# Attention and two feed-forward layers on one core: two small inputs stand behind the keys, and SyncE issues nearly all loads

## The chip, the cores and the metric

The kernel runs on one core of a Trainium2 chip. Its time is the device time of one execution in microseconds (us); lower is better. Five engines work side by side, each through its own instructions in order: TensorE (PE; PEld is its weight load), VectorE (DVE), ScalarE (ACT), GpSimd (POOL) and SyncE (SP). Transfers between HBM and on-chip memory are issued by an engine's queue (SPq, ACTq) and carried by 16 DMA engines.

## What is computed

```python
# q, k, v: batch 2, 8 heads, 768 positions, 64 wide; n_sink = 4, window = 128
scores = q @ k.T / 8                 # per head
keep = (col < n_sink) | ((0 <= row - col) & (row - col < window))
a = softmax(where(keep, scores, -1e9))
x = (a @ v) as 1536 tokens x 512
h = x @ moe_w_in                     # 512 -> 2048
x = (maximum(h, 0) + alpha * minimum(h, 0)) @ moe_w_out
x = maximum(x @ moe2_w_in, 0) ** 2 @ moe2_w_out      # again 512 -> 2048 -> 512
```

`n_sink`, `window` (the run's two numbers) and `alpha` are inputs of the run.

## The kernel before

Tokens are cut into 12 chunks of 128 (6 to a batch). Attention runs as 24 jobs, two to a chunk (`g`: four heads each). A job is: scores on TensorE (L529), mask and minimum on VectorE (L542), exponentials on ScalarE (L546), normalising (L562 on VectorE or L561 on ScalarE), transposes (L571), sums with the values (L604), and the result split into a high and a low fp32r part in `X` (L240, L247). The masks are made once, in `masks()`, from `parf`, the float copy of the run's two numbers.

A weight tile (`w`) is a half of 512 columns; packed it is 512 KB. The keys of a chunk are 320 KB, its values 256 KB, its queries 256 KB (or 128 KB a job). It arrives packed in a `raw` buffer (or in a part of `Y0` that serves as one), is unpacked by VectorE (L285, L287, L290) with a correction from ScalarE (L281), and split into `w`'s two parts (L240, L247). The first eight input halves (`w0` to `w7`) are wanted while attention runs; the feed-forward products of the first layer (L309, L341) begin between attention jobs. Both layers' products follow to the end.

`Plan` takes every step with a due number, its reads and writes and an estimated cost for each engine that could do it, and lists the steps by simulating that; each engine then runs its own list in order. `Plan({...})` at L694 holds the time at which each engine is thought to be free first, and each transfer carries a cost (the `"dma"` numbers). Transfers signal on eight semaphores that are taken in turn, and a transfer is issued only when the one that had its semaphore before has landed. So a queue (and the engine whose queue it is) can stand still ahead of a transfer.

Before, the keys of the first four chunks and the first two weight halves are issued by ScalarE (L276, L512), the rest by SyncE. `par` (two 64-bit numbers, copied to 128 partitions) and `alpha` are transfers of their own (L426, L707). Until the products begin, 34 identity products (`WARM`, L712) are spread over TensorE's list.

Of the kernel before, what the change touches and what calls it, by code (L numbers as in the profile page):

```python
# [8 lines left out]
F32 = mybir.dt.float32  # L9
# [9 lines left out]
P = 128  # L19
# [150 lines left out]
@with_exitstack  # L170
def attn_moe_moe(ctx, tc, q, k, v, vsink, par, alpha, w1, w2, out):
    nc = tc.nc
# [19 lines left out]
    const = pool_of(ctx, "const")  # L192
    al = const.tile([P, NF], F32, name="al")
    oma = const.tile([P, NF], F32, name="oma")
    flag = const.tile([1, 8], F32, name="flag")
    slow = const.tile([1, 1], I32, name="slow")
    parf = const.tile([P, 4], F32, name="parf")
    pari = const.tile([P, 4], I32, name="pari")
    X = const.tile([P, 2, KT, NTOK], F32R, name="X")
# [52 lines left out]
    class Feed:  # L252
# [9 lines left out]
        def half(self, due, layer, f, slot, a, need):  # L262
            add, new = self.plan.add, self.places.new
            wk = f"w{slot}_{a}"
            w = self.w[layer, f, a] = new(wk)
            q = self.halves
            self.halves += 1
            r, more = self.raws(q)
            early = RAW_LOADS[q:q + 1] if self.early else ()
            rk, ck, xk = f"raw{r}", f"cs{q % 2}", f"x{q % 2}"  # L270
            cs, x = new(ck), new(xk)
            raw = new(rk) if r < 4 else lambda: Y[0][:, (r - 4) * 1024:(r - 3) * 1024].bitcast(U32).rearrange(
                "p (j w) -> p j w", w=2)
            src = (w1, w2)[layer][f, :, a * 512:(a + 1) * 512].bitcast(U32).rearrange("p (j w) -> p j w", w=2)
            at = due - PARTS + a
            by = nc.scalar if early and q < 2 else nc.sync  # L276
            add(early[0] if early else due - LOAD + a, more, [rk], ("dma", 1456, lambda: by.dma_start(out=raw(), in_=src)))
# [122 lines left out]
    class Short:  # L400
# [18 lines left out]
        def masks(self):  # L419
            con = self.con  # L420
            self.K = [con.tile([P, NG, 2, KC], F32, name=f"K{i}") for i in range(4)]
            self.early = self.places.new("g7")

            self.queries(0)
            self.keys(0, 0, nc.scalar)
            nc.sync.dma_start(out=pari, in_=par.bitcast(I32).rearrange("(o n) -> o n", o=1).to_broadcast([P, 4]))  # L426
            self.ident = con.tile([P, P], F32, name="ident")
# [21 lines left out]
            nc.vector.scalar_tensor_tensor(out=mrel, in0=past, scalar=float(P), in1=rel, op0=ALU.mult, op1=ALU.add)  # L449
            nc.vector.tensor_copy(out=parf, in_=pari)  # L450
            nc.vector.tensor_scalar(nosink, col, ns_f, None, op0=ALU.is_ge)
# [4 lines left out]
            nc.vector.scalar_tensor_tensor(out=self.mask0, in0=past2, scalar=BIG, in1=nosink,  # L456
                                           op0=ALU.mult, op1=ALU.mult)

            def others():
# [22 lines left out]
        def keys(self, i, place, by):  # L482
            by.dma_start(out=self.K[place].rearrange("p g a n -> p g (a n)"), in_=k[divmod(ORDER[i], NCH)])

# [3 lines left out]
        def values(self, due, at, key, src):  # L488
            t = self.places.new(key)
            self.load(due, [key], t, src, 728)  # L490
            self.v[at] = t, key

        def job(self, i, b, c, g):
# [9 lines left out]
            if i < 4:  # L503
                qk, qt = ("g", 7, i // 2, 0), lambda: halves(self.early()[:, i // 2, g * 256:g * 256 + 256].bitcast(F32))
                if g == 0:
                    add(due - AHEAD, [], [qk, ("g", 7, i // 2, 2)], ("dma", 690, lambda: i and self.queries(i // 2)))
            else:
                qk, qt = ring("q", 2)
                self.load(due - AHEAD, [qk], qt, halves(q[b, c, :, g]), 364)
            if g == 0:  # L510
                add(due - AHEAD, [], [("K", here)], ("dma", 862, lambda: i and self.keys(
                    i // NG, here, nc.scalar if i < 4 else nc.sync)))  # L512
                self.values(VALUE_LOADS.get(ci, due - 4), (b, c), f"v{here}", v[b, c * P:(c + 1) * P, :])
# [9 lines left out]
            def scores():  # L523
                for p in range(2):

                    for x, y, at in ((0, KC, before), (KC, W3, here)) if c else ((0, P, here),):
                        for j in range(2):
                            rows = slice(j * D, (j + 1) * D)
                            nc.tensor.matmul(s()[:, 2 * p + j, x:y], lhsT=qt()[rows, p], rhs=K[at][rows, g, p, 0:y - x],  # L529
                                             start=True, stop=True)  # L530
# [84 lines left out]
    def full_attention():  # L615
        with ExitStack() as ctx:
# [22 lines left out]
            for c in range(NCH):  # L639
# [9 lines left out]
                for b in range(B):  # L649
                    for h in range(2 * 4):  # L650
# [6 lines left out]
                        for cc in range(NCH):  # L657
                            nc.sync.dma_start(out=kt[:, cc * P:(cc + 1) * P],
                                              in_=k[b, cc, :, g].rearrange("p (a s) -> p a s", a=2)[rows, pr % 2, 0:P])
                            nc.sync.dma_start(out=vv[:, cc], in_=v[b, cc * P:(cc + 1) * P, pr * 2 * D:(pr + 1) * 2 * D])  # L660
# [32 lines left out]
    with tc.manual_schedule():  # L693
        plan = Plan({"pe": 2500, "dve": 4500, "pool": 1500, "act": 2100, "dma": 800})  # L694
        places = Places()
# [10 lines left out]
        att.masks()  # L706
        plan.add(0, [], ["al"], ("dma", 56, lambda: nc.sync.dma_start(out=al, in_=alpha)))  # L707
        plan.add(0, ["al"], ["oma"], ("dve", 85, lambda: nc.vector.tensor_scalar(oma, al, -1.0, 1.0, op0=ALU.mult, op1=ALU.add)))
        att.start()
# [151 lines left out]
```

## Time and profile before

| | |
|---|---|
| median of 3 runs | 638.97 us (638.12 to 639.36) |
| the profiled execution | 638.03 us, of which 636.3 us are its span |
| TensorE busy | 618.6 us, 97% of the span |
| VectorE, ScalarE, GpSimd busy | 388.8, 253.0, 29.1 us |
| granted TensorE clock, mean | 0.993 |

The span runs from the first to the last instruction; 1.7 us of the execution lie outside it. The rows below come from the profiled execution, and their times count from the start of the span. A product on TensorE is pipelined and its end is modelled, so "busy" says only that TensorE had one under way.

### The profile page before, as it was taken

How to read it: one execution, taken by the hardware profiler on the slowest of the kernel's cores; microseconds unless marked ns; L12 is line 12 of the kernel's file. 1: busy time of each engine (PE TensorE's matmuls, PEld its weight loads, DVE VectorE, ACT ScalarE, POOL GpSimd, SP SyncE). 2: the span in 40 equal slices, each digit the busy share in tenths (PEclk: the TensorE clock that was granted, in tenths of full speed). 3: DMA queues.
4: the chain of work that ended last, by engine and by line, in shares of the span. 5: the costliest groups of instructions: out<-in, count | busy, mean ns of one | idle time of the engine just before them, and what ended most of it. 6: DMA issues, size and time to landing. Idle time of an engine off the chain costs nothing.

```text
span 636.3 us, 9094 instructions
## 1 busy us (share of the span) xinstructions
PE 618.6 (97%) x3448; PEld 512.7 (81%) x3448; DVE 388.8 (61%) x924; ACT 253.0 (40%) x591; POOL 29.1 (5%) x48
## 2 busy tenths in 40 slices
PE   5989999999999999999999999999999999999996
PEld 4778877878888888788888888888888888888885
DVE  3999997667755949554289993333396424434342
ACT  2888985556654725321045671111262201010110
POOL 0012112121100000000000000000000000000000
PEclk9889999999999999999999999999999999999999
DMA  8465233210262435200005540000040000100102
GB/s 311 163 237 172 85 100 93 92 39 26 79 221 66 133 98 167 67 1 1 0 4 176 193 141 18 1 0 1 0 133 1 2 0 1 67 0 21 46 1 71
DMA packets 18340, 48.13 MB, mean 76 GB/s; under 512 B 2288, under 2 KB 5104, under 8 KB 18288
## 3 DMA queue, kind: packets, MB, share of 16 engines
q1 hardware_dynamic: 17568, 45.63, 21.7%
q10 hardware_dynamic: 720, 1.84, 0.7%
q8 instruction: 29, 0.48, 0.3%
q14 instruction: 23, 0.19, 0.1%
HBM read 44.31 MB, written 3.15 MB: 75 GB/s over the span
## 4 chain that ended last, share of the span: by engine, by line
PE 88%; DVE 9%; DMA 2%; ACT 0%; issue 0%; SPq 0%; DVEq 0%
PE h L309 38%; PE yb L341 31%; PE h L341 10%; PE o L604 4%; PE s L529 3%; PE t L571 1%; DMA raw<-w 1%; DVE x L290 1%; DVE sp L542 1%; DVE w L247 1%; DVE r L321 1%; DVE x L287 1%; PE h L712 1%; DMA v<-v 1%; DVE g L247 1%; DVE s L536 1%
## 5 line engine op out<-in xcount | busy, mean ns | idle before, releaser
L309 PE MATMUL h<-X,w 128*128 128x512 f32 (+1 forms) x1248 | 275.1, 375 | 0.1
L309 PEld LDWEIGHTS h<-X,w 128*128 128x128 f32 x1248 | 221.6, 188 | 42.4 <-DVE r L321 0.3
L341 PE MATMUL yb<-w,g 128*128 128x512 f32 x576 | 134.5, 389 | 0.0
L341 PEld LDWEIGHTS yb<-w,g 128*128 128x128 f32 x576 | 108.1, 188 | 22.4
L326 DVE TENSOR_TENSOR r<-r 128x512 f32<-128x512 f32 x48 | 33.2, 691 | 122.8 <-ACT r L324 122.8
L324 ACT ACTIVATE r<-h 128x512 f32<-128x512 f32 x48 | 28.7, 598 | 174.5 <-PE h L309 174.3
L341 PE MATMUL h<-g,w 128*128 128x512 f32 x288 | 69.5, 394 | 0.4 <-DVE r L321 0.3
L247 DVE TENSOR_TENSOR g<-r,g 128x512 fp32r<-128x512 f32 (+1 forms) x104 | 68.1, 655 | 2.2
L341 PE MATMUL yb<-g,w 128*128 128x512 f32 x288 | 68.6, 391 | 0.1
L341 PEld LDWEIGHTS yb<-g,w 128*128 128x128 f32 x288 | 53.7, 188 | 12.4 <-DVE g L247 1.4
L341 PEld LDWEIGHTS h<-g,w 128*128 128x128 f32 x288 | 53.2, 188 | 12.1 <-DVE r L321 0.8
L321 DVE SCALAR_TENSOR_TENSOR r<-r,oma,h 128x512 f32<-128x512 f32 (+1 forms) x56 | 37.2, 665 | 37.9 <-ACT r L319 37.7
L319 ACT ACTIVATE r<-h 128x512 f32<-128x512 f32 (+1 forms) x56 | 29.7, 531 | 59.2 <-PE h L309 58.8
L281 ACT ACTIVATE cs<-raw 128x512 f32<-128x512 f32 x56 | 37.4, 673 | 35.0 <-DVE x L290 25.6
L290 DVE SCALAR_TENSOR_TENSOR x<-cs,x 128x512 uint32<-128x512 uint32 x64 | 43.9, 693 | 2.0 <-ACT x L283 0.3
L247 DVE TENSOR_TENSOR w<-x,w 128x512 fp32r<-128x512 f32 x64 | 44.5, 697 | 1.1
L546 ACT ACTIVATE sp<-sp,nm 128x160 f32<-128x160 f32 (+1 forms) x96 | 39.8, 417 | 11.8 <-DMA Y<-w 8.2
L240 DVE CAST g<-r 128x512 fp32r<-128x512 f32 (+1 forms) x67 | 28.1, 420 | 2.7
L240 DVE CAST w<-x 128x512 fp32r<-128x512 f32 x26 | 11.1, 425 | 28.6 <-PE h L309 18.4
L287 DVE TENSOR_SCALAR x<-raw 128x512 uint16<-128x512 uint16 x56 | 26.2, 471 | 0.1
L240 ACT CAST w<-x 128x512 fp32r<-128x512 f32 x38 | 23.4, 617 | 6.3 <-DVE x L290 5.6
L529 PE MATMUL s<-K,q 64*128 64x160 f32 (+1 forms) x320 | 25.2, 297 | 0.4 <-DVE nm L542 0.4
(84 smaller groups left out, 466.2 us busy)
## 6 DMA issues: line engine op xcount, KB each, us to landing
raw<-w SPq DMA_DIRECT2D x54, 512.0 KB, 3.7
Y<-w SPq DMA_DIRECT2D x8, 512.0 KB, 5.3
K<-k SPq DMA_DIRECT2D x10, 320.0 KB, 3.9
v<-v SPq DMA_DIRECT2D x12, 256.0 KB, 3.3
out<-Y SPq DMA_DIRECT2D x11, 256.0 KB, 2.1
q<-q SPq DMA_DIRECT2D x20, 128.0 KB, 2.2
raw<-w ACTq DMA_DIRECT2D x2, 512.0 KB, 6.8
K<-k ACTq DMA_DIRECT2D x2, 320.0 KB, 4.8
```

The lines of the kernel that those rows point to most:

```text
L240: return lambda: f(**dict(zip(("out", "in_"), get())))
L247: nc.vector.tensor_tensor(out=lo, in0=src, in1=hi.bitcast(F32), op=ALU.subtract)
L281: add(at, [rk], [ck], ("act", 560, lambda: nc.scalar.activation(out=cs(), in_=raw()[:, :, 1].bitcast(F32), func=AF.Abs, scale=2.0 ** -112)))
L287: add(at, [rk], [(xk, 0)], ("dve", dve_ns(512, True), lambda: nc.vector.tensor_scalar(half(U16, 0), raw().bitcast(U16).rearrange("p j (w a ...
L290: add(at, [ck, *two(xk)], two(xk), ("dve", dve_ns(512), lambda: nc.vector.scalar_tensor_tensor(out=x(), in0=cs().bitcast(U32), scalar=3, i ...
L309: nc.tensor.matmul(like(h()[:, 0:n], xs), lhsT=wi()[:, a, kt * P:(kt + 1) * P], rhs=xs, start=kt == 0 and i == 0, stop=kt == KT - 1 and i ...
L319: add(SOON + due, [hk], [rk], ("act", act_ns(n, True), lambda: nc.scalar.activation(out=rs(), in_=hs(), func=AF.Relu, scale=-1.0)))
L321: add(SOON + due, [hk, rk, "oma"], [rk], ("dve", dve_ns(n + 60), lambda: nc.vector.scalar_tensor_tensor(out=rs(), in0=rs(), scalar=oma[:, ...
L326: add(SOON + due, [rk], [rk], ("dve", dve_ns(n), lambda: nc.vector.tensor_tensor(out=rs(), in0=rs(), in1=rs(), op=ALU.mult)))
L341: nc.tensor.matmul(y(), lhsT=lhsT, rhs=rhs, start=first and i == 0, stop=last and i == 2)
L529: nc.tensor.matmul(s()[:, 2 * p + j, x:y], lhsT=qt()[rows, p], rhs=K[at][rows, g, p, 0:y - x], start=True, stop=True)
L546: ("act", act_ns(n) + 190, lambda h=h: nc.scalar.activation(out=sp()[:, h, 0:n], in_=sp()[:, h, 0:n], func=AF.Exp, scale=-1.0, bias=nm()[: ...
```

## The change

`par` and `alpha` are no longer inputs of their own. The host copies the four 32-bit words of the two numbers and the 16 columns of `alpha` behind the 640 keys of each row of `k`, and the first load of keys (`K0`) takes 660 columns where the others take 640. `parf` and `oma` (1 - alpha) are read from there; `oma` is now made inside `masks()`. Of all loads, ScalarE issues the first keys alone; the other keys and the first two weight halves go to SyncE's list. Five cost numbers of transfers are lowered, and the planner takes VectorE to be free at 5500 instead of 4500 and the transfers at 400 instead of 800.

```diff
-    al = const.tile([P, NF], F32, name="al")
-    pari = const.tile([P, 4], I32, name="pari")
...
-            by = nc.scalar if early and q < 2 else nc.sync
-            add(..., ("dma", 1456, lambda: by.dma_start(out=raw(), in_=src)))
+            add(..., ("dma", 1330, lambda: nc.sync.dma_start(out=raw(), in_=src)))
...
-            self.K = [con.tile([P, NG, 2, KC], F32, name=f"K{i}") for i in range(4)]
+            self.K = [con.tile([P, 4 * KC + (0 if i else 4 + NF)], F32, name=f"K{i}") for i in range(4)]
             self.queries(0)
             self.keys(0, 0, nc.scalar)
-            nc.sync.dma_start(out=pari, in_=par.bitcast(I32)....to_broadcast([P, 4]))
...
-            nc.vector.tensor_copy(out=parf, in_=pari)
+            more = self.K[0][:, 4 * KC:]
+            nc.vector.tensor_copy(out=parf, in_=more[:, 0:4].bitcast(I32))
...
+            nc.vector.tensor_scalar(oma, more[:, 4:], -1.0, 1.0, op0=ALU.mult, op1=ALU.add)
...
-            by.dma_start(out=self.K[place]..., in_=k[divmod(ORDER[i], NCH)])
+            n = self.K[place].shape[1] if i == 0 else 4 * KC
+            by.dma_start(out=self.K[place][:, 0:n], in_=k[divmod(ORDER[i], NCH)][:, 0:n])
...
-                    i // NG, here, nc.scalar if i < 4 else nc.sync)))
+                    i // NG, here, nc.sync)))
...
-        plan = Plan({"pe": 2500, "dve": 4500, "pool": 1500, "act": 2100, "dma": 800})
+        plan = Plan({"pe": 2500, "dve": 5500, "pool": 1500, "act": 2100, "dma": 400})
...
-        plan.add(0, [], ["al"], ("dma", 56, ...))
-        plan.add(0, ["al"], ["oma"], ("dve", 85, ...))
```

The other costs: values 728 to 655, the first queries 690 to 655, keys 862 to 820.

SyncE's list from its start, before (`g7` holds the first queries, `raw` and `Y0` packed weight halves):

```order
L479 DMA g7_93<-q 128x512
L426 DMA pari_63<-par 128x4
L479 DMA g7_93<-q 128x512
L486 DMA v0_148<-v 128x512
L486 DMA v1_169<-v 128x512
L277 DMA raw2_183<-w1 128x1024
L277 DMA Y0_65<-w1 128x1024 x2
L486 DMA q0_263<-q 128x256
```

and after:

```order
L477 DMA g7_91<-q 128x512 x2
L482 DMA K1_88<-k 128x640
L274 DMA raw0_125<-w1 128x1024
L485 DMA v0_138<-v 128x512
L274 DMA raw1_140<-w1 128x1024
L485 DMA v1_153<-v 128x512
L274 DMA raw2_167<-w1 128x1024
L274 DMA Y0_63<-w1 128x1024 x2
L485 DMA q0_238<-q 128x256
```

`K1`, `raw0` and `raw1` have come in ahead of the values, and `pari` is gone. ScalarE's list from its start, before:

```order
L483 DMA K0_89<-k 128x640
L441 ACT_TABLE_LOAD
L441 ACTIVATE flag_60<-ident_97 1x1
L483 DMA K1_90<-k 128x640
L277 DMA raw0_131<-w1 128x1024
L277 DMA raw1_150<-w1 128x1024
L546 ACTIVATE sp0_154,sm0_158<-sp0_154,nm0_155 128x128 x4
L281 ACTIVATE cs0_185<-raw0_131 128x512
```

and after:

```order
L482 DMA K0_87<-k 128x660
L437 ACT_TABLE_LOAD
L437 ACTIVATE flag_59<-ident_94 1x1
L545 ACTIVATE sp0_150,sm0_158<-sp0_150,nm0_151 128x128 x4
L278 ACTIVATE cs0_183<-raw0_125 128x512
```

Three transfers that stood ahead of the first exponentials have left this list. TensorE's list where the sums of the seventh and eighth jobs stand, before (the scores of `q1_456` begin the stretch):

```order
L529 MATMUL s_583<-K1_90,q1_456 128x160 x2
L529 MATMUL s_583<-K3_92,q1_456 128x128 x2
L529 MATMUL s_583<-K1_90,q1_456 128x160 x2
L529 MATMUL s_583<-K3_92,q1_456 128x128 x2
L577 MATMUL o_609<-ident_97,mask0_101 128x128
L604 MATMUL o_609<-ss0_615,vs0_418 64x128 x2
```

and after, with the same scores (`q1_442`):

```order
L528 MATMUL s_602<-K1_88,q1_442 128x160 x2
L528 MATMUL s_602<-K3_90,q1_442 128x128 x2
L528 MATMUL s_602<-K1_88,q1_442 128x160 x2
L528 MATMUL s_602<-K3_90,q1_442 128x128 x2
L306 MATMUL h1_568<-X_62,w3_0_453 128x256 x3
L576 MATMUL o_629<-ident_94,mask0_98 128x128
L306 MATMUL h1_568<-X_62,w3_0_453 128x256 x3
L306 MATMUL h0_640<-X_62,w4_0_554 128x256 x6
L603 MATMUL o_629<-ss0_646,vs0_392 64x128 x2
```

Products of the feed-forward (L306, before L309) now stand between the attention steps, here those of the fourth and fifth weight half.

## Rows read from the trace of the kernel before

**Rows 1.** Stretches: length; busy us of PE, PEld, DVE, ACT, POOL; clock; DMA; GB/s

```profile
0.00:25.00 25.00, 17.05 (x111) 15.08 (x112) 13.02 (x67) 12.28 (x43) 1.14 (x8) 0.93 0.69 253
25.00:86.00 61.00, 56.93 (x550) 49.76 (x549) 59.59 (x194) 53.01 (x160) 11.39 (x14) 0.97 0.47 156
...
170.00:636.30 466.30, 460.88 (x2030) 380.26 (x2028) 255.22 (x446) 138.62 (x229) 0.00 (x0) 1.00 0.18 58
```

**Rows 2.** Shorter stretches, the same columns

```profile
10.00:15.00 5.00, 1.71 (x12) 1.46 (x12) 0.17 (x1) 1.82 (x9) 0.00 (x0) 1.00 1.04 404
15.00:20.00 5.00, 3.51 (x21) 3.29 (x21) 4.30 (x19) 4.32 (x15) 0.00 (x0) 0.66 0.90 345
20.00:25.00 5.00, 5.00 (x45) 4.29 (x44) 4.62 (x24) 4.65 (x19) 0.00 (x0) 1.00 0.02 5
...
40.00:45.00 5.00, 2.87 (x33) 2.34 (x31) 5.00 (x14) 4.11 (x12) 1.46 (x2) 0.85 0.51 166
```

**Rows 3.** Timeline, TensorE: start, duration, operation, [idle before <-what ended it]

```profile
3.17 2.93 PE L712 MATMUL h<-ident 128*128 128x128 f32 x12 [3.17 <-POOL ident L442]
...
6.02 1.23 PE L529 MATMUL s<-K,g 64*128 64x128 f32 x8
...
7.18 2.07 PE L712 MATMUL h<-ident 128*128 128x128 f32 x8
...
9.18 0.79 PE L529 MATMUL s<-K,g 64*128 64x128 f32 x8
...
9.90 1.80 PE L712 MATMUL h<-ident 128*128 128x128 f32 x12
...
16.49 1.22 PE L529 MATMUL s<-K,g 64*128 64x128 f32 x8 [4.78 <-DVE nm L542]
...
17.64 2.07 PE L712 MATMUL h<-ident 128*128 128x128 f32 x8
...
25.29 0.90 PE L529 MATMUL s<-K,q 64*128 64x160 f32 x10
...
42.94 0.33 PE L577 MATMUL o<-ident,mask 128*128 128x128 f32 x1 [1.53 <-DVE X L247]
```

**Rows 4.** Timeline, VectorE, the same columns

```profile
5.91 0.17 DVE L450 CAST parf<-pari 128x4 f32<-128x4 int32 x1 [3.73 <-DMA pari<-par]
...
8.11 0.28 DVE L542 CUSTOM_DVE_ANT_0 sp<-s,mask 128x128 f32<-128x128 f32 x1
...
8.95 0.08 DVE L542 DVE_READ_ACCUMULATOR2_ANT nm<- 128x1 f32 x1
...
14.83 0.46 DVE L285 TENSOR_SCALAR x<-raw 128x512 uint16<-128x512 uint16 x1 [5.79 <-DMA raw<-w]
...
15.51 0.28 DVE L542 CUSTOM_DVE_ANT_0 sp<-s,mask 128x128 f32<-128x128 f32 x1
...
20.20 0.29 DVE L542 CUSTOM_DVE_ANT_0 sp<-s,mask 128x128 f32<-128x128 f32 x1 [0.82 <-PE t L571]
```

**Rows 5.** Timeline, ScalarE and its queue (ACTq), the same columns

```profile
7.97 2.90 ACTq L277 DMA_DIRECT2D raw<-w  x2
...
10.92 0.40 ACT L546 ACTIVATE sp<-sp,nm 128x128 f32<-128x128 f32 x1 [8.17 <-DMA Y<-w]
```

**Rows 6.** Chain of waits, first 20 us: start, duration, what

```profile
2.67 5.28 DMA v<-v
...
7.97 6.83 DMA raw<-w
```

**Rows 7.** Transfers issued in 0 to 5.5 us: queue, count, size, us to landing

```profile
g<-q SPq DMA_DIRECT2D x2, 256.0 KB, 4.1
...
K<-k ACTq DMA_DIRECT2D x1, 320.0 KB, 3.5
...
pari<-par SPq DMA_DIRECT2D x1, 2.0 KB, 4.6
```

**Rows 8.** A stretch just after the first landings, columns as in Rows 1

```profile
4.00:4.70 0.70, 0.70 (x5) 0.70 (x5) 0.00 (x0) 0.00 (x0) 0.00 (x0) 1.00 0.79 68
```

More of the change, by code (lines that the diff above doesn't have):

```diff
@@ L170, in attn_moe_moe @@
 @with_exitstack
-def attn_moe_moe(ctx, tc, q, k, v, vsink, par, alpha, w1, w2, out):
+def attn_moe_moe(ctx, tc, q, k, v, vsink, w1, w2, out):
     nc = tc.nc
@@ L275, in half @@
             at = due - PARTS + a
-            by = nc.scalar if early and q < 2 else nc.sync
-            add(early[0] if early else due - LOAD + a, more, [rk], ("dma", 1456, lambda: by.dma_start(out=raw(), in_=src)))
+            add(early[0] if early else due - LOAD + a, more, [rk], ("dma", 1330, lambda: nc.sync.dma_start(out=raw(), in_=src)))
             half = lambda dt, j: x().bitcast(dt).rearrange("p (j w) -> p j w", w=2)[:, :, j]
@@ L425, in masks @@
             self.keys(0, 0, nc.scalar)
-            nc.sync.dma_start(out=pari, in_=par.bitcast(I32).rearrange("(o n) -> o n", o=1).to_broadcast([P, 4]))
             self.ident = con.tile([P, P], F32, name="ident")
@@ L482, in keys @@
         def keys(self, i, place, by):
-            by.dma_start(out=self.K[place].rearrange("p g a n -> p g (a n)"), in_=k[divmod(ORDER[i], NCH)])
+            n = self.K[place].shape[1] if i == 0 else 4 * KC
+            by.dma_start(out=self.K[place][:, 0:n], in_=k[divmod(ORDER[i], NCH)][:, 0:n])
         def load(self, due, keys, get, src, cost, by=nc.sync):
@@ L489, in values @@
             t = self.places.new(key)
-            self.load(due, [key], t, src, 728)
+            self.load(due, [key], t, src, 655)
             self.v[at] = t, key
@@ L505, in job @@
                 if g == 0:
-                    add(due - AHEAD, [], [qk, ("g", 7, i // 2, 2)], ("dma", 690, lambda: i and self.queries(i // 2)))
+                    add(due - AHEAD, [], [qk, ("g", 7, i // 2, 2)], ("dma", 655, lambda: i and self.queries(i // 2)))
             else:
@@ L510, in job @@
             if g == 0:
-                add(due - AHEAD, [], [("K", here)], ("dma", 862, lambda: i and self.keys(
-                    i // NG, here, nc.scalar if i < 4 else nc.sync)))
+                add(due - AHEAD, [], [("K", here)], ("dma", 820, lambda: i and self.keys(
+                    i // NG, here, nc.sync)))
                 self.values(VALUE_LOADS.get(ci, due - 4), (b, c), f"v{here}", v[b, c * P:(c + 1) * P, :])
@@ L528, in scores @@
                             rows = slice(j * D, (j + 1) * D)
-                            nc.tensor.matmul(s()[:, 2 * p + j, x:y], lhsT=qt()[rows, p], rhs=K[at][rows, g, p, 0:y - x],
+                            nc.tensor.matmul(s()[:, 2 * p + j, x:y], lhsT=qt()[rows, p], rhs=K[at][rows, (2 * g + p) * KC:(2 * g + p) * KC + y - x],
                                              start=True, stop=True)
@@ L658, in full_attention @@
                             nc.sync.dma_start(out=kt[:, cc * P:(cc + 1) * P],
-                                              in_=k[b, cc, :, g].rearrange("p (a s) -> p a s", a=2)[rows, pr % 2, 0:P])
+                                              in_=k[b, cc, rows, pr * KC:pr * KC + P])
                             nc.sync.dma_start(out=vv[:, cc], in_=v[b, cc * P:(cc + 1) * P, pr * 2 * D:(pr + 1) * 2 * D])
@@ L706, in attn_moe_moe @@
         att.masks()
-        plan.add(0, [], ["al"], ("dma", 56, lambda: nc.sync.dma_start(out=al, in_=alpha)))
-        plan.add(0, ["al"], ["oma"], ("dve", 85, lambda: nc.vector.tensor_scalar(oma, al, -1.0, 1.0, op0=ALU.mult, op1=ALU.add)))
         att.start()
@@ L840, in weights @@
         return np.concatenate([a, w_out.reshape(ff // P, P, dm)], axis=2)
+    more = np.concatenate([np.broadcast_to(np.array([inputs["n_sink"], inputs["window"]], np.int64).view(np.float32), (P, 4)),
+                           np.asarray(inputs["moe_alpha"]).reshape(-1, P).T], axis=1)
+    kh = kh.reshape(b, c, P, 4 * KC)
+    kh = np.concatenate([kh, np.broadcast_to(more, (b, c) + more.shape)], axis=-1)
     arrays = {
         "q": heads(q).reshape(b, c, P, 2, 2 * P),
-        "k": kh.reshape(b, c, P, 2, 2 * KC),
+        "k": kh,
         "v": v.transpose(0, 2, 1, 3).reshape(b, s, h * d),
         "vsink": vs.transpose(0, 2, 3, 1, 4, 5).reshape(b, P, 2 * 4 * d),
-        "par": np.array([inputs["n_sink"], inputs["window"]], np.int64),
-        "alpha": np.asarray(inputs["moe_alpha"]).reshape(-1, P).T,
         "w1": weights(np.asarray(inputs["moe_w_in"]), np.asarray(inputs["moe_w_out"])),
```

## The prediction

> **What bounds the kernel now.** I read the stretches first. From 170 us on TensorE is as good as full, 460.88 of 466.30 us [rows 1]; between 25 and 86 us it is VectorE that is full, 59.59 of 61 us, with TensorE at 56.93 [rows 1]. The hole is at the front: in the first 25 us TensorE is busy for 17.05 and VectorE for 13.02 [rows 1], and between 10 and 15 us VectorE works for 0.17 us while the DMA engines are full at 404 GB/s [rows 2]. After 25 us VectorE's list has almost no air in it, and TensorE's work hangs on it until TensorE is itself full. So a microsecond that VectorE wins ahead of 25 us should come through to the end, and one won by another engine should not.
>
> The timeline of VectorE names what it waits for. It waits 3.73 us for `pari`, and then, with the first job's minima done at 9.03 (8.95 + 0.08), 5.79 us for the first weight half, which it unpacks at 14.83 [rows 4]. The chain of waits shows why that half is late: `raw0` is issued at 7.97, when a load of values has landed, and takes 6.83 us [rows 6]. It stood on ScalarE's queue, behind a semaphore that the values had, and its data then came behind loads that SyncE had issued meanwhile. The same queue holds up ScalarE: it waits 8.17 us and does its first exponential at 10.92, with two weight halves issued just before it [rows 5], though the minima were there from 9.03 on. The order of issue, not a lack of bandwidth, makes `raw0` late: in the first 25 us 6.3 MB land (253 GB/s [rows 1]), and the half megabyte that was wanted at 9 is not among the first ones.
>
> **The transfers, part by part.** `K0` and the first queries land as before, at about 4.3 us: issued at 0.81 (the first thing on either queue), 3.5 us to landing for the keys [rows 7]. `K0` grows from 320 to 330 KB, which at 404 GB/s [rows 2] is 0.03 us. `pari`, 2 KB in 4.6 us [rows 7], goes: while it was under way the engines moved 68 GB/s at a DMA share of 0.79 [rows 8]. `parf` can be made at 4.4 instead of 5.91.
>
> SyncE now issues queries, queries, `K1`, `raw0`. After the first pair, landed at 4.3, three loads lie up to the end of `raw0`: 256 + 320 + 512 KB, 1.11 MB, at 404 GB/s 2.8 us, so `raw0` lands at about 7.1. For the upper bound I take the 0.7 us at 68 GB/s [rows 8] as if it recurred twice: 8.5. `raw1` has 768 KB more in front of it and lands 1.9 us later, at 9.0 (10.4). Either is early enough, as follows. Moving the three loads to SyncE puts them ahead of the first values, by about 0.4 us of issue and 2 us of data each; the values are first wanted by the sums, which come after the transposes that VectorE waits for at 20.20 [rows 4], and that cover is 14 us even if all moves 6 us up. From `raw2` on each load must wait for the one eight places before it, and these land from 4.3 us on; the queue stays fed. ScalarE loses three issues ahead of its exponentials, so these can start as soon as the minima exist.
>
> **VectorE's first microseconds.** With `parf` at 4.4 the masks take the 2.2 us from 5.91 to 8.11 [rows 4], and `oma` adds one small operation of the size of `parf`'s cast, 0.17: ready at 6.8. The first scores are now the later ones. TensorE's list has ten identity products' rows ahead of them instead of twelve: (6.02 - 3.17)/12 = 0.24 us each [rows 3], so the scores start at 5.55 and end after 1.23 us, at 6.8. The minima take 0.92 us (8.11 to 9.03) and end at 7.7. VectorE then finds `raw0` landed (7.1), or waits to 8.5, unpacks it in 0.7 us, and wants the second job's scores. These are the next hurdle: ten rows of identity products follow the first scores, 0.25 us each by the eight between 7.18 and 9.18 [rows 3]; from 6.7 that is 9.2, and scores of 0.79 us [rows 3] end at 10.0. So the second job's minima start at 10.1 against 15.51 [rows 4]: **5.4 us earlier**. Even the late bound for `raw0` (8.5 + 0.7) is covered by that wait for TensorE.
>
> **The next wait.** At 20.20 VectorE waits 0.82 us for TensorE's transposes [rows 4]. They stood behind eight rows of identity products that took 2.07 us, where twelve took 1.80 a little earlier [rows 3]. (The rows at 3.17 and 7.18 are as slow, and the recorded clock gives no reason there; I have used them as they are.) The granted clock is 0.66 in the slow stretch and 1.00 in the one before [rows 2], which is the lower level of 1.2 GHz for a part of it, after 4.78 us in which TensorE stood still [rows 3]. That standstill is the wait for `raw0` again, so I let both go: at 0.15 us a row the eight take 1.2, and 0.8 us of the wait goes, **0.8 us**. From there on the order is the old one up to about 25 us. The loads that are wanted then (third keys, third queries) are the 12th and 11th of SyncE's list: from 4.3 us on 4.2 MB lie up to their end, at 404 GB/s they land by 14.7, and they are wanted by the scores that start at 25.29 today [rows 3], so at 19.
>
> **The middle.** The new costs change the order between 25 and 170 us: weight halves and feed-forward products come earlier and stand between attention steps. The amount of work stays: VectorE's list is two instructions shorter, and some casts and copies change places with ScalarE's. I take 0 for it. The bounds: in 25 to 86 us TensorE is idle 4.1 us and VectorE 1.4 [rows 1]. Half of TensorE's lies in one hole, 2.1 us at 40 to 45 [rows 2], of which 1.53 is the wait of an L577 for VectorE [rows 3], just where products now stand in between. VectorE is full there, so only its own 1.4 us and about 1 us of work handed to ScalarE can be gained: -2.4. Against it, new waits in a list ordered differently: four of the size of the 0.82 us wait [rows 4], +3.3.
>
> **Sum.** 5.4 + 0.8 + 0 = 6.2 us. The profiled execution, 638.03 us (636.3 of span and 1.7 around it), becomes 631.8; the median of the runs, 0.94 us above it, becomes **632.8**.
>
> **Rivals.** 1. *The middle gives a part back.* Attention now shares TensorE's and VectorE's lists with more products, and a step that waits holds all behind it. With the +3.3 of above or somewhat more the time is 634.5 to 638. For it: the order changes at nearly every step. Against: the lists put ready work in the gaps.
> 2. *The hole at 40 us closes too*, with the 2.4 us of above: 629 to 631. For it: the products between L529 and L577 in the new list. Against: VectorE is full all through that hole.
> 3. *The order of issue is worth nothing.* If the first weight half landed no earlier than now (the DMA engines are full, with a share of 1.04 and 0.90 between 10 and 20 us [rows 2]), VectorE would stand as it does and the time would be 638 to 640. Against it: the row of `raw0`'s issue at 7.97 [rows 6]; 2 MB of loads that are wanted later (two of values, three weight halves) are issued first today. The Trainium skill (DMA: Bandwidth & Descriptors, Issuing engines are not separate DMA queues) says that loads started from several engines run on the same 16 DMA engines and that spreading them saves only issue time; by that rule alone, taking three of them off ScalarE's queue gains nothing and costs SyncE three issues. The rows agree that bandwidth is not the point, but they show a cost that the rule leaves out, a queue standing still for a semaphore.
> 4. *Slower: the feed-forward holds attention up.* TensorE works in order, and the new list has products of `w1` to `w4` ahead of scores and transposes. If these wait for VectorE's split of a weight half, the scores behind them are late, VectorE has no minima to make, and makes the next weight half later still. Each such turn costs VectorE what the transposes cost it today, 0.82 us [rows 4]. To end above 640.3 it takes (6.2 + 1.3)/0.82, ten such turns. Against it: today's list has products between the jobs too, and all waits together cost VectorE 1.4 us in the 61 from 25 to 86 [rows 1].
>
> **How the numbers follow.** A difference of 0.2%, 1.3 us, is about what a measurement of this kernel can tell from none. Chances: the forecast (631 to 634.5) 0.60, rival 1 0.18 (a little of it within 1.3 us), rival 2 0.11, rival 3 0.06, rival 4 0.05. The range goes from 629.3 to 637.3: it holds the forecast, rival 2 but for its edge, and most of rival 1. Faster 0.87, same 0.08, slower 0.05.
>
> **What would show it.** VectorE's first L285 (now L282) near 8 us and never above 9; the second job's minima near 10; ScalarE's first exponential within 0.4 us of the first minimum; no TensorE gap of over 2 us after 3.2; the granted clock at 1.00 from about 10 us on. The stage from 86 us on should be as long as now, only 6 us earlier. The prediction is wrong if `raw0` lands after 10, if VectorE's idle time between 20 and 80 us is over 4 us, or if the gain is there at 25 us and gone at 170.

## The result and the profile after

The changed kernel takes 630.71 us (median of 4 runs, 629.88 to 631.33) against 638.56 us (638.12 to 639.36) for the kernel before on the same chip: a ratio of 0.9875, 95% interval 0.9858 to 0.9892. The gain is 7.9 us where 6.2 were forecast. A second set of runs of the same kernel gave 631.27 us, ratio 0.9887 (0.987 to 0.9903). The profiled execution took 630.62 us with a span of 628.9.

VectorE's timeline (start, duration, operation, [idle before <-what ended it]) answers [rows 4]:

```profile
4.61 0.17 DVE L447 CAST parf<-K 128x4 f32<-128x4 int32 x1 [2.43 <-DMA K<-k]
...
6.89 0.28 DVE L541 CUSTOM_DVE_ANT_0 sp<-s,mask 128x128 f32<-128x128 f32 x1
...
9.39 0.47 DVE L282 TENSOR_SCALAR x<-raw 128x512 uint16<-128x512 uint16 x1 [1.58 <-DMA raw<-w]
...
10.09 0.28 DVE L541 CUSTOM_DVE_ANT_0 sp<-s,mask 128x128 f32<-128x128 f32 x1
...
13.68 0.28 DVE L541 CUSTOM_DVE_ANT_0 sp<-s,mask 128x128 f32<-128x128 f32 x1
```

The first minima start at 6.89 instead of 8.11, the second job's at 10.09 instead of 15.51, and the third job's at 13.68 instead of 20.20, without a wait ahead of them. ScalarE's first exponential follows the first minimum by 0.3 us, where before three transfers stood ahead of it [rows 5]:

```profile
7.21 0.40 ACT L545 ACTIVATE sp<-sp,nm 128x128 f32<-128x128 f32 x1 [4.47 <-DVE nm L541]
```

For a measure of the front as a whole I take the first feed-forward product on TensorE, here of the kernel before and then of the changed one:

```profile
31.61 2.52 PE L309 MATMUL h<-X,w 128*128 128x256 f32 x18
```

```profile
5.60 1.23 PE L528 MATMUL s<-K,g 64*128 64x128 f32 x8
...
8.67 0.72 PE L528 MATMUL s<-K,g 64*128 64x128 f32 x8
...
25.41 2.11 PE L306 MATMUL h<-X,w 128*128 128x256 f32 x15
```

It comes 6.20 us earlier. The measure of the end is ScalarE's issue of the last output, again before and after:

```profile
631.81 0.36 ACTq L384 DMA_DIRECT2D out<-Y  x1
```

```profile
623.68 0.36 ACTq L381 DMA_DIRECT2D out<-Y  x1
```

It comes 8.13 us earlier, so 1.93 us are won between 25 us and the end. The spans differ by 7.4 only, because 5.2 us lie behind that issue now and 4.5 before (636.3 - 631.81), which no step of the change touches (4.5 to 5.4 in all fourteen profiles). The stretches (length; busy time and instructions of PE, PEld, DVE, ACT, POOL; granted clock, DMA share, GB/s) answer [rows 1] and [rows 2]:

```profile
0.00:25.00 25.00, 21.09 (x176) 18.00 (x178) 19.33 (x89) 18.29 (x63) 1.13 (x8) 1.00 0.87 309
25.00:86.00 61.00, 57.68 (x584) 50.91 (x583) 60.59 (x198) 53.65 (x160) 12.75 (x18) 1.00 0.45 146
...
10.00:15.00 5.00, 4.83 (x40) 4.37 (x40) 5.00 (x27) 4.55 (x18) 0.00 (x0) 1.00 1.04 414
15.00:20.00 5.00, 5.00 (x51) 4.02 (x50) 4.97 (x20) 5.00 (x19) 0.00 (x0) 1.00 1.04 400
20.00:25.00 5.00, 4.42 (x49) 3.51 (x50) 4.76 (x18) 5.00 (x18) 0.00 (x0) 1.00 0.71 228
40.00:45.00 5.00, 4.90 (x56) 4.44 (x56) 5.00 (x16) 4.21 (x14) 1.53 (x2) 1.00 0.66 225
```

In the first 25 us VectorE works for 19.33 us instead of 13.02 and TensorE for 21.09 instead of 17.05. From 10 to 25 us VectorE is busy for 14.73 of 15 us, and so is ScalarE, for 14.55: two engines are full there now. The granted clock is 1.00 in each of these stretches, where it was 0.66 from 15 to 20 and 0.85 from 40 to 45. And the hole of 2.13 us at 40 us is gone: TensorE's longest standing still behind 25 us is 0.85 us now, at 45.5 us, where it was 1.53. How much idle time that saves in sum is asked below.

### The profile page after: what moved, and what is told of

Its sections match the earlier page's. It is cut to its first block, busy times and chain, and to the rows that moved or that the text cites. A ratio compares the mean times of both kernels' runs of the same rounds, so it can differ in the third digit from the quotient of the medians.

```text
span 628.9 us, 9085 instructions
## 1 busy us (share of the span) xinstructions
PE 615.1 (98%) x3448; PEld 509.8 (81%) x3448; DVE 385.4 (61%) x922; ACT 253.3 (40%) x596; POOL 28.4 (5%) x48
## 4 chain that ended last, share of the span: by engine, by line
PE 85%; DVE 7%; ACT 4%; DMA 2%; issue 0%; SPq 0%; DVEq 0%; ACTq 0%
PE h L306 38%; PE yb L338 31%; PE h L338 10%; PE o L603 3%; PE s L528 2%; DMA raw<-w 1%; PE t L570 1%; DVE x L284 1%; ACT sp L560 1%; DVE x L287 1%; ACT sp L545 1%; DVE sp L541 1%; DVE w L245 1%; DMA v<-v 1%; DVE r L318 1%; DVE g L245 1%
## 5 line engine op out<-in xcount | busy, mean ns | idle before, releaser
L306 PE MATMUL h<-X,w 128*128 128x512 f32 (+1 forms) x1248 | 276.4, 375 | 0.6 <-DVE r L318 0.6
L306 PEld LDWEIGHTS h<-X,w 128*128 128x128 f32 x1248 | 222.2, 188 | 43.2 <-DVE r L318 1.1
L238 DVE CAST g<-r 128x512 fp32r<-128x512 f32 (+1 forms) x71 | 29.4, 414 | 2.7
L238 ACT CAST w<-x 128x512 fp32r<-128x512 f32 x41 | 25.3, 616 | 9.1 <-DVE x L287 7.4
L238 DVE CAST w<-x 128x512 fp32r<-128x512 f32 x23 | 9.8, 426 | 29.2 <-PE h L306 18.9
```

What stands on the lines that cost most here:

```text
L238: return lambda: f(**dict(zip(("out", "in_"), get())))
L306: nc.tensor.matmul(like(h()[:, 0:n], xs), lhsT=wi()[:, a, kt * P:(kt + 1) * P], rhs=xs, start=kt == 0 and i == 0, stop=kt == KT - 1 and i ...
```

## The experiments

All times are medians beside runs of the kernel before on the same chip (638.55 to 638.97 us). "First product" and "last output" are the two measures of above, read from one profiled execution each, whose time lies up to 0.9 us from the median. The first product has the same number of TensorE's steps ahead of it in every list.

| kernel | us | ratio, 95% | first product | last output |
|---|---|---|---|---|
| before | 638.56 | | 31.61 | 631.81 |
| after | 630.71 | 0.9858 to 0.9892 | 25.41 | 623.68 |
| after, once more | 631.27 | 0.987 to 0.9903 | 25.71 | 624.15 |
| old costs, rest changed | 630.88 | 0.9861 to 0.9894 | 24.61 | 623.73 |
| new costs alone | 636.75 | 0.9952 to 0.9979 | 32.90 | 630.65 |
| loads on ScalarE's queue | 638.97 | 0.9997 to 1.0017 | 34.52 | 633.04 |
| inputs apart | 629.47 | 0.9842 to 0.9874 | 25.04 | 622.74 |
| loads first on ScalarE's queue | 633.77 | 0.991 to 0.9937 | 29.21 | 627.41 |
| raw0 late, from SyncE | 634.44 | 0.9926 to 0.9953 | 28.12 | 626.99 |
| VectorE + 1.3 us | 631.43 | 0.9878 to 0.9909 | 26.40 | 624.22 |
| ScalarE + 2.0 us | 631.95 | 0.9887 to 0.9917 | 26.90 | 624.90 |
| identity first | 631.36 | 0.9865 to 0.9895 | 25.77 | 624.82 |
| identity first, two loads first on ScalarE's queue | 630.18 | 0.9846 to 0.9877 | 25.68 | 623.24 |
| inputs apart, identity first | 631.20 | 0.9851 to 0.9884 | 26.25 | 624.13 |

The kernel once more was the yardstick for the others:

> The changed kernel as it is, for comparisons below a microsecond on one chip. All theories: 630 to 631.5 us, 0.987 of the kernel before.

**Which part of the change pays.** Four kernels undo or do one part.

```diff
-add(..., ("dma", 1330, lambda: nc.sync.dma_start(out=raw(), in_=src)))
+add(..., ("dma", 1330, lambda: (nc.scalar if early and q < 2 else nc.sync).dma_start(out=raw(), in_=src)))
...
-    i // NG, here, nc.sync)))
+    i // NG, here, nc.scalar if i < 4 else nc.sync)))
```

> The changed kernel with the second keys and the first two weight halves issued by ScalarE's queue again (packed inputs and new numbers kept). Theory (a queue that stands still ahead of a transfer is the cost): raw0 issued at 6 to 8 us, first exponential at 9 to 11 us, second job's minima at 13 to 15.5, 634.5 to 636.5 us. Rival (it doesn't matter which engine issues): first weight half near 9.4 as now, second job's minima near 10.1, 630.4 to 631.5 us.

Measured 638.97 us: putting the three transfers back on ScalarE's queue takes all of the gain, more than I expected (634.5 to 636.5). ScalarE's timeline and VectorE's:

```profile
5.17 0.33 ACTq L482 DMA_DIRECT2D K<-k  x1
9.11 3.70 ACTq L274 DMA_DIRECT2D raw<-w  x2
12.86 0.40 ACT L545 ACTIVATE sp<-sp,nm 128x128 f32<-128x128 f32 x1 [10.11 <-DMA K<-k]
```

```profile
16.21 0.46 DVE L282 TENSOR_SCALAR x<-raw 128x512 uint16<-128x512 uint16 x1 [8.39 <-DMA raw<-w]
```

The three are the second keys and the first two weight halves (of the keys, ScalarE issued those of two chunks before, not of four). Each stood on the queue for a semaphore; `raw0` was issued at 9.11 and unpacked at 16.21, the first exponential waited 10.11 us. This is the state of before, a little worse (7.97, 14.83 and 8.17 us there [rows 4, 5]).

The planner's numbers (four costs of transfers, not five, and two starting times), old in the changed kernel:

```diff
-            add(..., ("dma", 1330, lambda: nc.sync.dma_start(out=raw(), in_=src)))
+            add(..., ("dma", 1456, lambda: nc.sync.dma_start(out=raw(), in_=src)))
...
-            self.load(due, [key], t, src, 655)
+            self.load(due, [key], t, src, 728)
...
-                    add(..., ("dma", 655, lambda: i and self.queries(i // 2)))
+                    add(..., ("dma", 690, lambda: i and self.queries(i // 2)))
...
-                add(..., ("dma", 820, lambda: i and self.keys(
+                add(..., ("dma", 862, lambda: i and self.keys(
...
-        plan = Plan({"pe": 2500, "dve": 5500, "pool": 1500, "act": 2100, "dma": 400})
+        plan = Plan({"pe": 2500, "dve": 4500, "pool": 1500, "act": 2100, "dma": 800})
```

> The changed kernel with the planner's old numbers (1456, 728, 690, 862; VectorE free at 4500, transfers at 800), so packed inputs and SyncE's issues alone. Theory (the front gains 6.0 to 6.5 us, the order of the middle about 1.5 to 2 more by closing the hole at 40 us): second job's minima at 10 to 10.3 us as in the changed kernel, TensorE's idle time of over 1.5 us at 40 to 45 us back, 632 to 632.8 us. Rival (the order of the middle is worth nothing, all of the 7.9 us is front): 630.4 to 631.2 us.

and the same edit the other way round in the kernel before:

> The kernel before with the planner's new numbers alone; ScalarE's and SyncE's first lists stay as before. Theory (the numbers close the hole at 40 us by a new order, and the front is the transfers' alone): second job's minima at 15 to 16 us as before, TensorE's idle time at 40 to 45 us under 1 us instead of 2.1, 636.0 to 637.3 us. Rival (the hole belongs to the late front, not to the order): hole stays, 638.0 to 639.3 us.

The first gave 630.88 us: the theory's time was missed, and the new costs are worth nothing on top of the rest. (The first product comes 0.8 to 1.1 us earlier than in the changed kernel, which neither theory nor rival had.) The second gave 636.75 us: alone they are worth 2.2 us, as the theory had it. The two parts don't add up (7.9 alone and 2.2 alone make 7.6 to 7.9 together). What stands behind 25 us shows why. Here is the stretch at 40 us, first with the old costs in the changed kernel, then with the new costs in the kernel before, and the second's stretch from 25 us on:

```profile
40.00:45.00 5.00, 4.70 (x57) 4.21 (x57) 5.00 (x14) 4.50 (x14) 1.68 (x2) 1.00 0.68 261
```

```profile
40.00:45.00 5.00, 4.88 (x58) 4.24 (x57) 5.00 (x19) 4.32 (x15) 3.15 (x4) 1.00 0.12 41
25.00:86.00 61.00, 57.94 (x602) 51.55 (x599) 60.46 (x215) 56.06 (x173) 11.42 (x14) 1.00 0.44 150
```

The hole of 2.13 us is in neither, and the granted clock is 1.00 in both. The hole belongs to the one order that the kernel before has, and either part of the change makes another order. The rival of the second run, that the late front makes the hole, falls: its front is as late as before, with the second job's minima at 15.73.

The inputs, apart again as `par` and `alpha`:

```diff
+            nc.sync.dma_start(out=pari, in_=par.bitcast(I32)....to_broadcast([P, 4]))
-            nc.vector.tensor_copy(out=parf, in_=more[:, 0:4].bitcast(I32))
+            nc.vector.tensor_copy(out=parf, in_=pari)
...
+        plan.add(0, [], ["al"], ("dma", 56, lambda: nc.sync.dma_start(out=al, in_=alpha)))
```

> The changed kernel with the two numbers and alpha as transfers of their own again (order of issue and new numbers kept). Theory (the wait for TensorE's warm rows covers the first minima): parf at 5.7 to 6.2 us instead of 4.6, first minima at 8 to 8.3 instead of 6.9, second job's minima at 10.1 to 10.5, 630.7 to 631.3 us. Rival (the first minima set the front): everything 1.2 us later, 631.8 to 632.2 us.

```profile
5.83 0.17 DVE L449 CAST parf<-pari 128x4 f32<-128x4 int32 x1 [3.65 <-DMA pari<-par]
...
10.02 0.29 DVE L541 CUSTOM_DVE_ANT_0 sp<-s,mask 128x128 f32<-128x128 f32 x1 [0.36 <-PE s L528]
```

`parf` is 1.2 us later and the second job's minima are not: TensorE's rows cover it. So the packed inputs win nothing here. The time, 629.47 us, is 1.2 us below the theory's lower end and the lowest of all; every one of its runs (629.35 to 629.79) lies below every run of the changed kernel on that chip (630.69 to 631.59). The first product comes 0.4 to 0.7 us earlier and the last output 0.9 to 1.4: most of it is won behind the front, in an order that also differs there. Which place wins it was not separated.

This kernel and the kernel before with the new costs have the same list on every engine, and differ in who issues the three loads: 629.47 against 636.75 us, first product at 25.04 against 32.90. The changed kernel and the one with the loads on ScalarE's queue are such a pair as well: 631.27 against 638.97, 25.71 against 34.52. So with the lists held, and each run taken against the kernel before on its chip, moving the three loads is worth 7.1 us in one order and 7.7 in the other. The new costs add 2.2 us while the front is late and nothing once it is early.

**Is it the engine that issues, or the waiting?** In the changed kernel, with all lists kept, ScalarE was given the three transfers at the very start, and SyncE no longer issues them:

```diff
             self.keys(0, 0, nc.scalar)
+            self.keys(1, 1, nc.scalar)
+            for f in range(2):
+                nc.scalar.dma_start(out=FIRST_RAW[f](), in_=w1[f, :, 0:512]...)
```

> The changed kernel, every engine's list as it is, except that ScalarE issues the second keys and the first two weight halves, and does so right behind the first keys and ahead of its table load, where none of the eight semaphores is taken. Theory (the cost was the queue's standing still ahead of a transfer, and not the engine that issues): issues done by 2.7 us without a wait, raw0 landed by 8 to 10 us, first exponential near 7.3, second job's minima at 10 to 10.8, 630.5 to 631.8 us. Rival (ScalarE's queue is the slower one for these loads): second job's minima after 12, 632.5 to 636 us.

633.77 us, in the rival's range, but not for its reason: the third of them was the ninth transfer in all and stood for a semaphore, against what I had written. ScalarE's timeline, then TensorE's, then VectorE's:

```profile
1.73 3.28 ACTq L426 DMA_DIRECT2D raw<-w  x2
5.04 1.28 ACT L441 ACT_TABLE_LOAD   x1 [5.04 <-DMA K<-k]
```

```profile
6.96 2.50 PE L714 MATMUL h<-ident 128*128 128x128 f32 x10 [6.96 <-POOL ident L442]
9.39 1.23 PE L532 MATMUL s<-K,g 64*128 64x128 f32 x8
```

```profile
10.67 0.29 DVE L545 CUSTOM_DVE_ANT_0 sp<-s,mask 128x128 f32<-128x128 f32 x1 [3.60 <-PE s L532]
```

The table load came at 5.04 instead of 1.25; GpSimd's select waits for the activation behind it, and TensorE's first rows for the select. They started at 6.96 instead of 3.16, and the first product 3.5 to 3.8 us later. VectorE waited 3.60 us for TensorE's scores, and not at all for `raw0`, which it unpacked right behind the first minima, at 11.52 us: here the standing still cost 2.5 to 3.1 us without a late half. One load that waits on a queue held up three engines. Mended, with two transfers instead of three, and with the identity made ahead of the activation (the next edit), so that the queue waits for nothing:

```diff
             self.keys(0, 0, nc.scalar)
+            self.keys(1, 1, nc.scalar)
+            nc.scalar.dma_start(out=FIRST_RAW[0](), in_=w1[0, :, 0:512]...)
```

> As the kernel with the identity ready first (the run beside this one), except that ScalarE issues the second keys and the first weight half right behind the first keys, ahead of its table load; the eighth semaphore isn't reached by then. Theory (a queue costs what it stands still, whichever engine issues): three issues done by 2.2 us, no wait, raw0 landed by 8 to 9.5, second job's minima within 0.5 us of the other's, time within 0.8 us of the other's. Rival (these loads are slower from ScalarE's queue): second job's minima over 2 us later than the other's, 632 us or more.

```profile
0.81 0.89 ACTq L485 DMA_DIRECT2D K<-k  x2
1.73 0.45 ACTq L425 DMA_DIRECT2D raw<-w  x1
2.21 1.28 ACT L442 ACT_TABLE_LOAD   x1 [2.21 <-issue]
```

630.18 us, first product at 25.68 against 25.77 for its neighbour, the kernel with the identity first: for these two loads it is of no account in the front which engine issues, as long as its queue doesn't stand still. (The time is 1.2 us below the neighbour's, where I had allowed 0.8. The difference arises behind the front, in lists that are alike: the first products are 0.1 us apart, the last outputs 1.6. Its cause is open.) The Trainium skill (DMA: Bandwidth & Descriptors, Issuing engines are not separate DMA queues) says that loads run on the same 16 DMA engines whichever engine starts them, and that starting them from several saves only issue time. This run agrees; the two in which a load on ScalarE's queue stood for a semaphore (638.97 and 633.77 us) show what the rule leaves out.

**Is it the late weight half, or ScalarE's standing still?** Both were there before. Here SyncE alone issues, ScalarE's queue stays free, and `raw0` is last of the first eight loads (behind the values, `raw2` and `raw1`):

```diff
+            def issue(q):
+                if early and q < 2:
+                    HELD.append((raw, src))
+                    return
+                nc.sync.dma_start(out=raw(), in_=src)
+                if early and q == 2:
+                    for r, s in HELD[::-1]:
+                        nc.sync.dma_start(out=r(), in_=s)
```

> The changed kernel with SyncE alone issuing, but raw1 and raw0 behind the first values and raw2 (raw0 last of eight). Lists otherwise as they are, ScalarE's queue stays free. Theory (VectorE's wait for the first weight half was the cost): raw0 lands at 11.5 to 13, second job's minima at 12.2 to 13.8 instead of 10.1, first exponential still near 7.3, 632.8 to 634.8 us. Rival (ScalarE's standing still was the cost and the weight half is covered): 630.5 to 631.5 us.

ScalarE's timeline, then VectorE's:

```profile
7.33 0.40 ACT L556 ACTIVATE sp<-sp,nm 128x128 f32<-128x128 f32 x1 [4.59 <-DVE nm L552]
```

```profile
12.12 0.46 DVE L293 TENSOR_SCALAR x<-raw 128x512 uint16<-128x512 uint16 x1 [4.19 <-DMA raw<-w]
...
12.80 0.28 DVE L552 CUSTOM_DVE_ANT_0 sp<-s,mask 128x128 f32<-128x128 f32 x1
```

634.44 us, as the theory had it. With ScalarE on time, the half that lands 2.7 to 3.9 us later than in the changed kernel costs 2.4 to 2.7 us at the first product and 3.2 to 3.7 us in time. So a late half is a cost by itself. What ScalarE's late exponentials add to it in the kernel before was not run alone.

**Does a microsecond of VectorE count, and one of ScalarE not?** Three casts of 128x512 into a part of `X` that is written again later, on the one engine or the other, beside its work on `raw1` (at 12.5 and 12.4 us; the edit for VectorE is shown):

```diff
+            def extras():
+                for _ in range(3 if early and q == 1 else 0):
+                    nc.vector.tensor_copy(out=extra, in_=raw()[:, :, 1].bitcast(F32))
```

> The changed kernel with three added casts of 128x512 on VectorE (of a packed weight half into a part of X that is written again later) ahead of the unpacking of raw1, near 11 us: some 1.9 us of work for VectorE and nothing else. Theory (a microsecond of VectorE ahead of 25 us comes through): 1.5 to 2.1 us longer, 632.3 to 633.4 us. Rival (slack behind it swallows it): under 0.7 us longer, 630.7 to 631.7 us.

> The changed kernel with the same three casts on ScalarE, near 11 us: some 1.9 us of work for ScalarE and nothing else. Theory (a microsecond of another engine doesn't come through): 0 to 0.7 us longer, 630.7 to 631.7 us. Rival (ScalarE is as critical as VectorE in the front): 1.5 to 2.1 us longer, 632.3 to 633.4 us.

The casts and the first product of the run on VectorE, and the casts, VectorE's longest wait and the first product of the run on ScalarE:

```profile
12.53 1.35 DVE L280 CAST X<-raw 128x512 fp32r<-128x512 f32 x3
```

```profile
26.40 2.12 PE L311 MATMUL h<-X,w 128*128 128x256 f32 x15
```

```profile
12.39 2.07 ACT L280 CAST X<-raw 128x512 fp32r<-128x512 f32 x3
```

```profile
17.77 0.17 DVE L555 TENSOR_SCALAR rc<-sm 128x4 f32<-128x4 f32 x1 [1.64 <-ACT sp L550]
```

```profile
26.90 2.12 PE L311 MATMUL h<-X,w 128*128 128x256 f32 x15
```

VectorE got 1.27 us of work (3 x 0.42, less than the 1.9 I had reckoned), ScalarE 2.0 (3 x 0.67). The first product is 0.7 to 1.0 us later in the one and 1.2 to 1.5 in the other, the time 0.2 to 0.7 and 0.7 to 1.2 us longer. By its time the first run falls to its rival and the second lies between the two; the intervals of both overlap that of the changed kernel, so that the times alone are not clear of the noise. Neither theory holds: at the first product both engines count, each by somewhat over half, and the time follows by less. VectorE waits 1.64 us for ScalarE's exponentials.

**What is the next wait?** In the changed kernel GpSimd waits 1.27 us for the activation behind ScalarE's table load before it finishes the identity:

```profile
2.82 0.29 POOL L438 TENSOR_SCALAR_AFFINE_SELECT ident<-ident 128x128 f32<-128x128 f32 x1 [1.27 <-ACT flag L437]
```

One line moved:

```diff
-            nc.scalar.activation(out=flag[:, 0:1], in_=self.ident[0:1, 0:1], func=AF.Exp)
             nc.gpsimd.affine_select(out=self.ident, in_=self.ident, ...)
+            nc.scalar.activation(out=flag[:, 0:1], in_=self.ident[0:1, 0:1], func=AF.Exp)
```

> The changed kernel with one line moved: the activation that loads ScalarE's table reads the identity behind GpSimd's select instead of ahead of it, so that GpSimd no longer waits 1.27 us for it. Theory (the ten rows ahead of the second scores are the front's last wait): identity products start near 1.9 us instead of 3.16, first scores at 4.4 to 4.7, second scores at 7.9 to 8.3, second job's minima at 8.6 to 9.9 (raw0's landing sets it) instead of 10.1, 630.0 to 630.9 us. Rival (nothing ahead of the third job's minima counts any more): 630.9 to 631.6 us.

TensorE's first row, then VectorE's timeline:

```profile
1.97 1.44 PE L709 MATMUL h<-ident 128*128 128x128 f32 x5 [1.97 <-POOL ident L437]
```

```profile
9.66 0.29 DVE L541 CUSTOM_DVE_ANT_0 sp<-s,mask 128x128 f32<-128x128 f32 x1 [0.69 <-PE s L528]
...
13.86 0.29 DVE L541 CUSTOM_DVE_ANT_0 sp<-s,mask 128x128 f32<-128x128 f32 x1 [0.51 <-PE t L570]
```

631.36 us: nothing is won, the rival was right. TensorE starts 1.2 us earlier and the second job's minima 0.4, but VectorE then waits 0.51 us for the transposes and begins the third job's minima at 13.86, as in the changed kernel (13.68 and 13.80 in its two profiles). The same line in the kernel with the inputs apart:

> The kernel with the inputs apart, with the same line moved. There VectorE is done with the first minima and raw0 by 9.6 us, so 0.3 to 0.5 us can be won at the second job's minima: theory 629.0 to 629.5 us; rival (worth nothing, or the two chips' difference was all): 629.5 to 631 us.

```profile
9.12 0.72 PE L528 MATMUL s<-K,g 64*128 64x128 f32 x8 [1.54 <-DVE nm L541]
```

```profile
10.00:15.00 5.00, 5.00 (x32) 4.53 (x32) 3.56 (x17) 4.46 (x17) 0.00 (x0) 0.66 1.04 407
```

```profile
15.00 0.29 DVE L541 CUSTOM_DVE_ANT_0 sp<-s,mask 128x128 f32<-128x128 f32 x1 [1.44 <-PE t L570]
```

631.20 us, outside theory and rival, 1.7 worse than without the line (runs 628.89, 631.15, 631.26 and 631.41). In the profiled run TensorE finished its rows early and stood still for 1.54 us, waiting for VectorE; the granted clock from 10 to 15 us was 0.66 (the lower level of 1.2 GHz for a part of it), and the third job's minima came at 15.00, where they came at 13.79 without the line. One of the four runs escaped that loss, and two are as long as the profiled one with a mean clock as high as the short one's; what these lost is open. No version beat the one with the inputs apart, 629.47 us.

## Why the prediction was right, and where it was off

Time and sign were right and the range held. The front was right in the main, in part by luck, and one term was mis-sized, the middle. By its own steps:

- *The bound.* The hole at the front was the cost, as the stretches said. The rule that went with it, that a microsecond of VectorE ahead of 25 us comes through and one of another engine doesn't, falls: VectorE's came through in time by 0.2 to 0.7 us of 1.27, ScalarE's by 0.7 to 1.2 us of 2.0 (at the first product 0.7 to 1.0 and 1.2 to 1.5). I had read which engines were full from the kernel before, where ScalarE worked 12.28 us in the first 25 [rows 1]; once the hole is closed, it is full from 10 to 25 us too. The sum was not hurt, as I read it, since the change moved all three engines together; no run shows that.
- *The transfers.* `parf` came at 4.61 (4.4 said). `raw0` was unpacked at 9.39 where 7.1 was said, with 8.5 as the late bound: too early by the whole range. In the second profile of the same kernel it was unpacked at 8.19, within the bounds. Between the two the rate from 5 to 10 us differs, 297 GB/s in the first profile and 350 in the second, against the 404 I had used for it:

```profile
5.00:10.00 5.00, 5.00 (x35) 4.26 (x34) 3.28 (x21) 2.26 (x9) 0.00 (x0) 1.00 0.96 297
0.00:9.39 9.39, 6.23 (x37) 5.51 (x37) 4.00 (x25) 3.14 (x10) 1.13 (x8) 1.00 0.76 241
```

```profile
5.00:10.00 5.00, 5.00 (x31) 4.21 (x29) 3.65 (x21) 2.20 (x9) 0.00 (x0) 1.00 1.02 350
```

  The sum also took the loads to come one after the other. By 9.39 us 2.26 MB had moved (241 GB/s), where all loads up to `raw0` are 1.71 MB: the rest was data of loads issued behind it.
- *VectorE's first microseconds, 5.4 us.* Measured 15.51 - 10.09 = 5.42. The cover named for it was TensorE's rows ahead of the second scores. In the second profile that is what VectorE waits for, 1.05 us, and the minima start at 10.04; in the first the rows ran faster, and `raw0` itself set the start. Two different last waits, 0.05 us apart. The late half used up the cover, none was left: with `raw0` 0.9 us past its late bound, the 5.4 was met by luck in the first profile, and by the wait that I had named in the second.

```profile
8.19 0.46 DVE L282 TENSOR_SCALAR x<-raw 128x512 uint16<-128x512 uint16 x1 [0.18 <-DMA raw<-w]
...
10.04 0.29 DVE L541 CUSTOM_DVE_ANT_0 sp<-s,mask 128x128 f32<-128x128 f32 x1 [1.05 <-PE s L528]
```

- *The next wait, 0.8 us.* Third job's minima 6.52 us earlier, 1.10 more than the second's; the wait is gone, and the granted clock is 1.00 from 10 to 25 us. In the run with the three loads put back TensorE stood still for 7.49 us and the clock fell again:

```profile
15.00:20.00 5.00, 2.13 (x12) 1.91 (x13) 3.01 (x15) 3.46 (x11) 0.00 (x0) 0.50 1.00 399
```

  The third job's minima moved by 6.52 and 6.40 us in the two profiles, the first product by 6.20 and 5.90, against the sum of 6.2. That is nearer than the sum earned: it took the order up to 25 us as the old one, and the new order itself puts the first product 0.8 to 1.1 us later (24.61 with the old costs, 7.00 earlier than before).
- *The middle, taken as 0: the term that was mis-sized.* It gave 1.93 us (1.76 in the second profile). I had put the closing of the hole at 40 us (rival 2, chance 0.11) against the argument that VectorE is full through it. But what the hole cost was less its idle time than the clock behind it. From the first product to the last output, before and then after, and the stretch behind the hole before:

```profile
31.61:631.81 600.20, 595.20 (x3270) 492.74 (x3268) 369.52 (x837) 236.47 (x535) 28.00 (x40) 1.00 0.21 67
```

```profile
25.41:623.68 598.27, 593.60 (x3270) 491.57 (x3268) 365.65 (x833) 234.60 (x534) 27.25 (x40) 1.00 0.20 67
```

```profile
45.00:50.00 5.00, 5.00 (x49) 4.38 (x47) 4.04 (x14) 3.52 (x12) 1.68 (x2) 0.81 0.29 100
```

  TensorE is busy for 595.20 and 593.60 us with the same 3270 products, and idle for 5.00 and 4.67. So 1.60 of the 1.93 us are products that ran faster, and 0.33 are idle time: most of what the hole stood still came again in smaller waits. The clock was 0.85 from 40 to 45 us [rows 2] and 0.81 from 45 to 50, and 1.00 in the changed kernel; by an estimate from these two rows, (0.15 + 0.19) x 5 = 1.7 us of full clock. I had the 0.85, and the 0.97 from 25 to 86 us [rows 1], and priced only idle time. Of the kernel before there is this one profile. In all thirteen other executions TensorE is busy for 593.1 to 593.7 us between the two measures, and they lie 597.6 to 599.1 us apart, 1.1 to 2.6 less than before. The nine with the changed kernel's own order spread over nearly all of that among themselves, by their idle time, so the 1.93 us is good to some 0.8.
- *Rivals.* 1 (the middle gives back) and 4 (feed-forward holds attention up) did not come: VectorE's idle time from 25 to 86 us fell from 1.41 to 0.41 us. 2 came on top of the forecast, by 1.9 of its 2.4 us, and its chance was too small; but it had counted on idle time and work handed over, and what came back was mostly the clock, so its number is right by luck. 3 (the order of issue is worth nothing) is refuted by the run with the loads put back, which loses everything.
- *What would show it.* The second job's minima near 10, the exponential within 0.4 us of the first minimum, no gap of over 2 us on TensorE and the clock at 1.00 all came. The first unpacking "near 8 and never above 9" did not come in one profile of two.

## What to carry to other kernels

A load on the queue of an engine that also computes can cost twice when it has to wait for a semaphore: the data is late (3.2 to 3.7 us here by itself), and so is all that stands behind it on that engine, and what waits for that (2.5 to 3.1 us by itself, where it was the table load). Look for the transfers issued late, not for the engine that issues them. When a hole is closed, read again which engines are full, and price the clock behind a hole beside its idle time: here 1.6 of 1.9 us were clock. Orders that a planner makes afresh differed by up to 2 us whatever the edit was for, so an edit is judged with the order kept, or by several orders.

## What was not expected of the hardware

- The first loads ran at 297 GB/s in one execution and at 350 in another of the same kernel (5 to 10 us), and 512 KB issued at 2.19 us were unpacked at 9.39 and 8.19 us. From 10 us on the rates agree, 414 and 411 GB/s.
- Ten rows of identity products from 6.75 us on took 1.99 us in one execution of the changed kernel and 2.50 in the other, with a recorded clock of 1.00 in both: the moment at which the rows become fast moves from run to run. The Trainium skill (TensorE: Matmul & The Clock Gate, What's actually happening) says that the moment at which TensorE's clock rises varies from run to run; the rows' times in the two profiles agree, and the recorded clock doesn't show it.
- TensorE's standing still for 1.54 us from 7.57 us on was followed by a granted clock of 0.66 from 10 to 15 us (with the inputs apart and the identity first); 2.28 us from 11.5 on, in the run with `raw0` late, by 1.00 in the stretches from 10 to 20 us. The length alone does not tell.
- Executions with the same first product and the same lists behind it end up to 1.6 us apart (last output at 623.24 and 624.82, first products at 25.68 and 25.77), so single differences of that size say nothing about the middle.
